# Second MLP product of tiles 0 to 7 as seven block products per tile pair

## The chip, the cores and the metric

The kernel runs on one core of a Trainium2 chip. The metric is device time in microseconds of one execution, as the median of several runs. The core has a matrix engine (TensorE, PE in the profile, with its weight loads listed as PEld), VectorE (DVE), ScalarE (ACT), GpSimd (POOL) and SyncE (SP, which issues DMAs). Each engine works through its own queue in order; semaphores make one engine wait for another. Matmuls write to PSUM, which is used here in banks of 512 fp32 values per partition; all other data lies in SBUF.

## The reference, cut to what matters

Two parts work on the same normalized input: an attention block with cached keys and values, and an MLP mixer whose output gates the attention.

```python
xn = _layernorm(x)                                  # 2048 x 512
s  = attention(xn, k_cache, v_cache, wq, wo)        # 32 heads, Dh 128, 2048 keys
# mixer on xn:
h  = _gelu(_layernorm(xn) @ w1)                     # then shifted by rows, in four column groups
x1 = xn + shifted(h) @ w2
h2 = _gelu(_layernorm(x1) @ w3) @ w4                # 512 -> 1792 -> 512
g  = _silu(x1 + h2)
return x + s * g
```

The product with `w4` is the second MLP product of the title. Its input has 2048 rows of 1792 values, its output 2048 rows of 512.

## The kernel before, in words

All tokens are cut into 16 tiles of 128 rows; four tiles make a chunk of 512 rows. `xall` holds the tiles' running values (x, then x1, then x1 + h2, then the gate) in bf16, tile by tile.

The order of the work is written out by hand: every instruction goes through `pin(...)`, which keeps the program's order on its engine, and the tile framework adds the semaphore waits from reads and writes of tiles. A PSUM tile fills a bank (or half of one), and an access of one engine to it waits for the other engines' accesses to the same tile, whichever half they touch. No planner with costs or due times takes part in the stage of the change.

The program begins with the mixer. It normalizes and transposes the tiles, then runs `m1` (product with w1, gelu), `m2` (shifted product with w2) and `x1` (adding it into `xall`), `ln2` (second normalization, on VectorE, with a DMA transpose into `xn2T`), and then the MLP:

- `m3(c, f)` makes 256 of the 1792 hidden columns of chunk `c`, transposed: eight matmuls of 512 columns into one two-bank PSUM tile, then one gelu on ScalarE into `h2`. Seven calls make a chunk.
- `m4(t, ps, fcs)` makes the second MLP product of tile `t`: for each of 14 blocks of 128 hidden columns one matmul, with the block of `h2` (128 x 128) as weights and the matching 128 rows of `w4` (512 columns) streamed. It sums in one PSUM bank.
- `x2` adds that bank into `xall` on VectorE. `gate_tanh` takes tanh of half of it on ScalarE, and `gate_silu` multiplies on VectorE.

The stage runs as: `m3` of chunks 0 and 1, then `gate_out` (m4, x2, tanh, silu) of tiles 0 to 3, `m3` of chunk 2, `gate_out` of tiles 4 to 7, `m3` of chunk 3. During this SyncE issues the loads of w4, of the first keys and values and of the first output weights `wo`. The pool `pL` is then closed and its memory goes to `pB`, which holds `wo` and the attention's tiles. The second product of tiles 8 to 15 follows one matmul at a time inside the attention's first slots (`held_mm`, with the same `m4`).

The rest, over a thousand microseconds, is the attention: per unit (head and 512 queries) eight slots of score matmuls, exp on ScalarE, value matmuls, and sums of exp on VectorE. The projection of queries there already uses seven block products in place of eight (`w_sum`, `x_sum`, `product`, `q_take`, `q_part`), whose rows of the profile serve as prices in the prediction.

In the profile every matmul carries line 112, that of the helper `mm`, so matmuls are told apart by the tiles they write and read: `ps_o<-w_sb,h2T` is the second MLP product of tiles 0 to 7, `ps_m<-w_sb,h2T` that of tiles 8 to 15, and `ps_s<-xn2T,w_sb` is `m3`. Line 293 is the gelu of `m3`, 302 is `x2`, 306 is tanh, 310 is the silu, 219 a normalization, 796 the load of `w4`, 516 that of `wo`. In the query projection line 405 is a ScalarE copy of the first block product, and lines 413 to 421 are VectorE adds; 442 to 455 are the attention's sums of exp.

Of the kernel before, what the change touches and what calls it, by code (L numbers as in the profile page):

```python
# [8 lines left out]
ACT = mybir.ActivationFunctionType  # L9
ALU = mybir.AluOpType  # L10
FP32 = mybir.dt.float32
BF16 = mybir.dt.bfloat16
# [5 lines left out]
def kernel(  # L18
# [15 lines left out]
    nc = tc.nc  # L34
    P = nc.NUM_PARTITIONS
# [3 lines left out]
    Sq, D = x2d.shape  # L39
    _, H, Sk, Dh = A_k_cache.shape  # L40
# [5 lines left out]
    DC = D // P  # L46
    KC = Sk // P
    FC = F // P
# [11 lines left out]
    PADW = 8  # L60
    PSUM = bass.MemoryType.PSUM
    pin = tc.keep_in_program_order

    def pool(name, bufs=1, space=None, **kw):
        if space is not None:
            kw["space"] = space
        return tc.tile_pool(name=name, bufs=bufs, **kw)
# [4 lines left out]
    xall = const.tile([P, NT, D], BF16, name="xall")  # L72
# [22 lines left out]
    psO = ent(pool("psO", 2, PSUM))  # L95
    psX = ent(pool("psX", 1, PSUM))
# [4 lines left out]
    pR = right.enter_context(pool("pR", side="right", reuse_waits="tile"))  # L101
    left = ExitStack()
    pL = left.enter_context(pool("pL", reuse_waits="tile"))
# [7 lines left out]
    def mm(out, lhsT, rhs, start, stop, **kw):  # L111
        pin(nc.tensor.matmul(out=out, lhsT=lhsT, rhs=rhs, start=start, stop=stop, **kw))  # L112
# [8 lines left out]
        out=ident[:], in0=diag[:], scalar1=0.0, scalar2=None, op0=ALU.is_equal))  # L121
# [9 lines left out]
    kTs, vBs, wqs, wos, oTs, st = {}, {}, {}, {}, {}, {}  # L131
# [37 lines left out]
    def token(early, name):  # L169
        if early:  # L170
            return pL.tile([P, D], BF16, tag="xi", bufs=5, name=name)
        return tokp.tile([P, D], BF16, tag="ta", bufs=6, name=name)
# [9 lines left out]

    w1_sb = pL.tile([P, DC, D], BF16, name="w1_sb")
    w2_sb = pL.tile([P, DC, D], BF16, name="w2_sb")
    w3_sb = [pL.tile([P, DC, 2 * P], BF16, name=f"w3_sb{i}") for i in range(FC // 2)]
    hT = pL.tile([P, DC, Sq + PADW], BF16, name="hT")
    xn2T = {}
    w4_sb = [pR.tile([P, D], BF16, name=f"w4_sb{i}") for i in range(FC)]  # L190
    h2 = {}

    def power(out, ve):
# [74 lines left out]
    def m2(t, pl=psO, tag="ps_o"):  # L268
        ps = pl.tile([P, D], FP32, tag=tag, name="ps_o")
        for jc in range(DC):  # L270
            c0 = BASE_J[jc] + t * P - SHIFT[jc]
            mm(ps[:], hT[:, jc, c0:c0 + P], w2_sb[:, jc, :], jc == 0, jc == DC - 1)
        return ps
# [12 lines left out]
    def m3(c, f):  # L286
        ps = psS.tile([P, 2, 512], FP32, name="ps_s")
        for j in range(2):
            for dc in range(DC):
                mm(ps[:, j, :], w3_sb[f][:, dc, j * P:(j + 1) * P], xn2T[c][:, dc, :],  # L290
                   dc == 0, dc == DC - 1)
        h2[c, f] = pR.tile([P, 2, 512], BF16, tag="h2T", bufs=FC, name="h2T")
        pin(nc.scalar.activation(out=h2[c, f][:], in_=ps[:], func=ACT.Gelu_apprx_tanh))  # L293

    def m4(t, ps, fcs):
        c, ts = divmod(t, 4)
        for fc in fcs:
            mm(ps[:], h2[c, fc // 2][:, fc % 2, ts * P:(ts + 1) * P], w4_sb[fc][:],
               fc == 0, fc == FC - 1)

    def x2(t, ps):
        pin(nc.vector.tensor_tensor(out=xall[:, t, :], in0=ps[:], in1=xall[:, t, :], op=ALU.add))

    def gate_tanh(t):
        th = token(False, "th")
        pin(nc.scalar.activation(out=th[:], in_=xall[:, t, :], func=ACT.Tanh, scale=0.5))
        return th

    def gate_silu(t, th):
        pin(nc.vector.scalar_tensor_tensor(  # L310
            out=xall[:, t, :], in0=th[:], scalar=1.0, in1=xall[:, t, :], op0=ALU.add, op1=ALU.mult))
# [29 lines left out]
    def x_block(qt, half, dcs):  # L341
        c = qt * 512 + 256 * half
        return xnT[:, dcs, c:c + 256]
# [23 lines left out]
    def product(v, k):  # L367
        g, qt, hh = units[v]
        h = g * HG + hh
        s = sw.setdefault(v, {})  # L370
        if k in (1, 7):
            s["ps"] = psX.tile([P, 2, 256], FP32, tag="xa", name="ps_q")
        w, o = wc[h], [wc[h][:, i] for i in range(4)]
        b11, _, b21, b22 = (wqs[h + j][:, d, :] for d in (LO, HI) for j in (0, 1))
        side, x, b = {
            1: (0, x_block(qt, 0, LO), b11),
            2: (0, x_block(qt, 0, HI), b21),
            3: (1, xs[qt, 3], b22),
            4: (0, x_block(qt, 1, HI), o[3]),
            5: (1, xs[qt, 0], o[0]),  # L380
            6: (1, xs[qt, 1], o[1]),
            7: (0, xs[qt, 2], o[2]),
        }[k]
        for dc in range(2):
            mm(s["ps"][:, side, :], b[:, dc, :], x[:, dc, :], k in (1, 7) and dc == 0, True, skip_group_check=True)
# [296 lines left out]
    for jc in range(DC):  # L682
        b = BASE_J[jc]
# [78 lines left out]
    for u in range(HG, 2 * HG):  # L762
        q_ahead(u)
    pend = [(3, m2(3))]
    wqs[H - 1] = pL.tile([P, DC, Dh], BF16, name="wq_e")
    pin(nc.sync.dma_start(out=wqs[H - 1][:], in_=wq_v[:, :, (H - 1) * Dh:]))
    for t in range(12, 16):
        ln1(t, tr_dma)
# [24 lines left out]
        elif t < 13:  # L793
            ln2(t - 5)
    for i in range(FC):
        pin(nc.sync.dma_start(out=w4_sb[i][:], in_=B_w4[i * P:(i + 1) * P, :]))
    for t in range(8, 12):
        stats(xall[:, t, :], mv2, rs2, t)
    for h in range(HG):
        load_k(h, range(KSPLIT))  # L800
        load_v(h, (0, 1))
        if h == 0:
            for f in range(FC // 2):
                m3(0, f)
            for t in range(12, 16):
                stats(xall[:, t, :], mv2, rs2, t)
            for t in range(8, 12):
                ln2(t)
        if h == 1:
            for f in range(FC // 2):  # L810
                m3(1, f)
            for t in range(12, 16):
                ln2(t)

    def gate_out(t):
        ps = psO.tile([P, D], FP32, tag="ps_o", name="ps_o")
        m4(t, ps, range(FC))
        x2(t, ps)
        gate_silu(t, gate_tanh(t))

    for t in range(0, 4):
        gate_out(t)
    for f in range(FC // 2):
        m3(2, f)
    for t in range(4, 8):
        gate_out(t)
    for f in range(FC // 2):
        m3(3, f)
    left.close()
    pB = left.enter_context(pool("pB", reuse_waits="tile"))  # L830

# [5 lines left out]
    for g in range(NG - 1):  # L837
        b = (g * QT + QT - 1) * HG
# [18 lines left out]
    def held_mm(n):  # L857
        for _ in range((4, 10)[n] if n < 2 else 3 if n < SPU + 2 else 2 if n < 2 * SPU else 1 + (n % SPU in (1, 5, 7))):
            if not held:
                return  # L860
            t, fc = held.popleft()
            if fc == 0:
                heldps[t] = psX.tile([P, 512], FP32, tag=("xa", "xm")[t % 2], name="ps_m")
            m4(t, heldps[t], (fc,))
            if fc == FC - 1:
                held_out(t, n)
# [34 lines left out]
    for v in pairs:  # L901
        a = (v - 2) * SPU
# [19 lines left out]
    for h in range(HG, H, 2):  # L922
        u = (h // HG) * QT * HG + (-4, -2)[h % HG // 2]
# [8 lines left out]
    for n in range(UB * SPU):  # L932
        u, p = divmod(n, SPU)
# [72 lines left out]
    n = UB * SPU  # L1006
    t0 = 4 * (QT - 1)
    ps, tb, yl, whole = {}, {}, {}, {}
# [25 lines left out]
    def pv_to(k):  # L1034
# [29 lines left out]
        out=diag[:], in0=diag[:], scalar1=0.0, scalar2=None, op0=ALU.is_equal))  # L1064
# [98 lines left out]
```

## Time and profile before

| | |
|---|---|
| median of 3 runs | 1235.81 us (1235.81 to 1235.9) |
| the profiled execution, whole | 1236.42 us |
| its span, first to last instruction | 1234.6 us |
| TensorE's granted clock | 1.0 |
| DMA moved | 107.75 MB, mean 87 GB/s |

The page lists for each engine its busy time and share of the span, then the granted clock in 40 slices, then the chain of work that ended last, by engine. A row of a group reads: line, engine, operation, tiles written and read, shapes, count, busy microseconds in all, mean nanoseconds of one, and the idle time ahead of it with the engine that ended it. A row of the timeline reads: start in the span, duration, engine, line, operation, tiles, count; equal instructions in a row are merged into one with their count. A row of the windows reads: window, its length, then busy time and count of PE, PEld, DVE, ACT and POOL, the granted clock, the DMA share and GB/s. The end of a matmul is modelled, and a matmul's listed duration overlaps the next one's.

### The profile page before, as it was taken

Reading aid. Unit: us, or ns where it says so; the run is one execution under the profiler, and the core shown is the slowest. Engines: PE = TensorE matmul, PEld = TensorE weight load, DVE = VectorE, ACT = ScalarE, POOL = GpSimd, SP = SyncE. Lnnn points to the kernel's source line nnn. Section 1 sums busy time; section 2 is a strip of 40 time slices with the busy share of each in tenths; the row PEclk is TensorE's granted clock in tenths of the full one; section 3 lists DMA queues with packets and bytes.
Section 4 is the critical chain, followed back from the end, with each engine's and each line's share of the span. In section 5 each row is a group of like instructions: output and inputs, shape, how many; then the busy total and the mean of one; then the engine's idle time right before and its main releaser. Section 6 shows DMA issues by size and latency. Waiting matters only on the chain.

```text
span 1234.6 us, 17534 instructions
## 1 busy us (share of the span) xinstructions
PE 1227.5 (99%) x6267; PEld 636.5 (52%) x6267; DVE 1030.1 (83%) x1647; ACT 1105.8 (90%) x1237; POOL 26.6 (2%) x75
## 2 busy tenths in 40 slices
PE   9999999999999999999999999999999999999998
PEld 6444444455555555555555555555555555555545
DVE  7712778899888888988889888888889999999997
ACT  6345999899999999999999999999999999999996
POOL 5300000000000000000000000000000000000000
PEclk9999999999999999999999999999999999999999
DMA  8661122664334423354243523543345424553342
GB/s 176 168 140 35 31 39 65 96 99 94 63 80 100 106 57 82 87 111 85 58 95 91 111 56 69 103 104 72 76 83 111 107 58 90 99 107 66 77 81 66
DMA packets 244056, 107.75 MB, mean 87 GB/s; under 512 B 194816, under 2 KB 227712, under 8 KB 243968
## 3 DMA queue, kind: packets, MB, share of 16 engines
q1 hardware_dynamic: 243408, 106.17, 41.5%
q8 instruction: 49, 0.80, 0.3%
q10 hardware_dynamic: 560, 0.46, 0.1%
q14 instruction: 39, 0.32, 0.1%
HBM read 67.50 MB, written 2.36 MB: 57 GB/s over the span
## 4 chain that ended last, share of the span: by engine, by line
PE 94%; DVE 3%; DMA 2%; ACT 1%; issue 0%; SPq 0%; DVEq 0%; ACTq 0%
PE ps_s L112 39%; PE ps_o L112 37%; PE ps_wo L112 8%; PE ps_q L112 8%; PE ps_m L112 2%; DMA tT<-acc 1%; DVE acc L447 1%; ACT pT L436 1%; DMA rb<-dr 0%; DMA xin<-in_A_x_dram 0%; DVE sm L485 0%; PE ps_oh L112 0%; DVE oT L509 0%; DVE acc L451 0%; DVE y L1025 0%
## 5 line engine op out<-in xcount | busy, mean ns | idle before, releaser
L436 ACT ACTIVATE pT<-ps_s 128x1024 bf16<-128x1024 f32 x1016 | 1016.2, 1025 | 56.8 <-PE ps_s L112 26.1
L112 PE MATMUL ps_s<-qT,kT 128*128 128x512 bf16 (+1 forms) x2064 | 609.3, 378 | 0.0
L112 PE MATMUL ps_o<-pT,vb 128*128 128x512 bf16 x1984 | 590.2, 379 | 0.0
L447 DVE TENSOR_TENSOR acc<-acc,pT 128x2048 bf16<-128x2048 bf16 x254 | 307.0, 1208 | 54.9 <-ACT pT L436 54.4
L112 PEld LDWEIGHTS <-kT 128*128 128x128 bf16 x2064 | 232.7, 113 | 151.3 <-issue 1.0
L112 PEld LDWEIGHTS <-vb 128*128 128x128 bf16 x1984 | 193.9, 98 | 216.6
L442 DVE TENSOR_TENSOR acc<-pT 128x2048 bf16<-128x2048 bf16 x127 | 155.4, 1224 | 38.4 <-ACT pT L436 35.5
L112 PE MATMUL ps_wo<-wo_h,oT 128*128 128x512 bf16 x496 | 186.3, 379 | 0.0
L451 DVE TENSOR_TENSOR acc<-acc 128x1024 bf16<-128x1024 bf16 x127 | 87.4, 688 | 2.5
L509 DVE TENSOR_TENSOR oT<-ps_o,rb 128x512 bf16<-128x512 f32 x127 | 86.6, 682 | 1.1 <-DMA rb<-dr 0.8
L485 DVE TENSOR_REDUCE sm<-tT 128x4 f32<-128x512 bf16 x124 | 83.9, 676 | 2.8 <-DMA tT<-acc 2.7
L112 PEld LDWEIGHTS <-oT 128*128 128x128 bf16 x528 | 51.4, 98 | 52.6 <-issue 0.6
L112 PEld LDWEIGHTS <-wc 128*128 128x128 bf16 x440 | 43.0, 98 | 54.1 <-issue 2.7
L571 DVE TENSOR_TENSOR sacc<-ps_wo,sacc 128x512 f32<-128x512 f32 x96 | 65.7, 684 | 0.0
L112 PEld LDWEIGHTS <-wq_h 128*128 128x128 bf16 x398 | 38.9, 98 | 46.3
L112 PE MATMUL ps_q<-xnT,wq_h 128*128 128x256 bf16 (+1 forms) x288 | 61.1, 298 | 0.4 <-DVE sacc L559 0.4
L421 DVE TENSOR_TENSOR qT<-ps_q,tq 128x512 bf16<-128x512 f32 x55 | 38.0, 692 | 23.3 <-PE ps_q L112 22.9
L455 DVE TENSOR_TENSOR acc<-acc 128x512 bf16<-128x512 bf16 x127 | 52.9, 417 | 0.5
L293 ACT ACTIVATE h2T<-ps_s 128x1024 bf16<-128x1024 f32 x28 | 28.6, 1023 | 25.9 <-PE ps_s L112 25.9
L112 PE MATMUL ps_s<-xn2T,w_sb 128*128 128x512 bf16 x224 | 48.8, 379 | 0.0
L112 PEld LDWEIGHTS <-w_sb 128*128 128x128 bf16 x368 | 33.5, 98 | 29.6
L112 PE MATMUL ps_q<-xs,wc 128*128 128x256 bf16 x246 | 47.0, 273 | 0.0
(102 smaller groups left out, 585.6 us busy)
## 6 DMA issues: line engine op xcount, KB each, us to landing
rb<-dr SPq DMA_DIRECT2D x127, 256.0 KB, 3.9
vb<-in_A_v_cache_dram SPq DMA_DIRECT2D x62, 256.0 KB, 3.0
wq_h<-in_A_wq_dram SPq DMA_DIRECT2D x32, 128.0 KB, 3.0
wo_h<-in_A_wo_dram SPq DMA_DIRECT2D x32, 128.0 KB, 2.5
w_sb<-in_B_w_dram SPq DMA_DIRECT2D x8, 256.0 KB, 5.0
kT<-in_A_k_cache_dram SPq DMA_TRANSPOSE x128, 2.8
xl<-in_A_x_dram SPq DMA_DIRECT2D x16, 128.0 KB, 3.0
dr<-rc SPq DMA_DIRECT2D x127, 2.0 KB, 1.4
```

The source lines that it names most:

```text
L112: pin(nc.tensor.matmul(out=out, lhsT=lhsT, rhs=rhs, start=start, stop=stop, **kw))
L293: pin(nc.scalar.activation(out=h2[c, f][:], in_=ps[:], func=ACT.Gelu_apprx_tanh))
L421: pin(nc.vector.tensor_tensor(out=s["q"][:, 1:3], in0=ps, in1=u.to_broadcast([P, 2] + list(u.shape[2:])), op=ALU.add))
L436: pin(nc.scalar.activation(out=s["pT"][-1][:, jj:jj + 2, :], in_=sps[:], func=ACT.Exp, scale=SCALE))
L442: pin(nc.vector.tensor_tensor(out=s["acc"][:], in0=s["pT"][0][:], in1=s["pT"][1][:], op=ALU.add))
L447: pin(nc.vector.tensor_tensor(out=a[:], in0=a[:], in1=st[u]["pT"][i][:], op=ALU.add))
L451: pin(nc.vector.tensor_tensor(out=a[:, 0:2, :], in0=a[:, 0:2, :], in1=a[:, 2:4, :], op=ALU.add))
L455: pin(nc.vector.tensor_tensor(out=a[:, 0, :], in0=a[:, 0, :], in1=a[:, 1, :], op=ALU.add))
L485: pin(nc.vector.tensor_reduce(out=sm[:], in_=s["tT"][:], axis=mybir.AxisListType.X, op=ALU.add))
L509: pin(nc.vector.tensor_tensor(out=to, in0=o, in1=rb, op=ALU.mult))
L571: pin(nc.vector.tensor_tensor(out=sa, in0=ps[:], in1=sa, op=ALU.add))
```

## The change

The second MLP product of tiles 0 to 7 is made for two tiles at a time, with four blocks on each side: the two tiles give the rows, the two 128-column halves of each hidden block give the inner halves (`k` = 0 and 1), and the left and right 256 columns of `w4` give the columns. Seven products of sums of blocks replace the eight products of blocks. The operand sums are made on VectorE: `t1` to `t4` from `w4` once, `s1` to `s4` from `h2` per pair (`h_sums`). Each product is seven matmuls of 256 columns that sum in PSUM; the products are then added up by eight VectorE adds and one copy on ScalarE per pair, which also bring in the residual from `xall`.

To be read in blocks, `w4` becomes one tile instead of 14, and `h2` one tile per chunk (two buffers) instead of 14 buffers of a seventh. The sums use memory whose first content is no longer needed: `hT` for the sums of `w4`, the `xp` buffers for the first pair of a chunk, and the `w1` and `w2` tiles for the second pair. For this some tiles get a tag. A pair's two fp32 work tiles, `mu` in the place of `wq_e` and `mt`, are used for nothing else at that time.

Within a pair the first product is copied by ScalarE after the second product has been issued into the other half of the same bank. For the second pair of a chunk, the gate of the first pair (two tanh, two silu) is issued between that copy and the pair's first add.

```diff
-    w1_sb = pL.tile([P, DC, D], BF16, name="w1_sb")
-    w2_sb = pL.tile([P, DC, D], BF16, name="w2_sb")
+    w1_sb = pL.tile([P, DC, D], BF16, tag="w1", bufs=1, name="w1_sb")
+    w2_sb = pL.tile([P, DC, D], BF16, tag="w2", bufs=1, name="w2_sb")
...
-    hT = pL.tile([P, DC, Sq + PADW], BF16, name="hT")
+    hT = pL.tile([P, DC, Sq + PADW], BF16, tag="hT", bufs=1, name="hT")
...
-    w4_sb = [pR.tile([P, D], BF16, name=f"w4_sb{i}") for i in range(FC)]
+    w4_sb = pR.tile([P, FC // 2, 2, D], BF16, name="w4_sb")
...
-        h2[c, f] = pR.tile([P, 2, 512], BF16, tag="h2T", bufs=FC, name="h2T")
-        pin(nc.scalar.activation(out=h2[c, f][:], in_=ps[:], func=ACT.Gelu_apprx_tanh))
+        if f == 0:
+            h2[c] = pR.tile([P, FC // 2, 2, 512], BF16, tag="h2T", bufs=2, name="h2T")
+        pin(nc.scalar.activation(out=h2[c][:, f], in_=ps[:], func=ACT.Gelu_apprx_tanh))
...
-            mm(ps[:], h2[c, fc // 2][:, fc % 2, ts * P:(ts + 1) * P], w4_sb[fc][:],
+            mm(ps[:], h2[c][:, fc // 2, fc % 2, ts * P:(ts + 1) * P], w4_sb[:, fc // 2, fc % 2, :],
...
-    wqs[H - 1] = pL.tile([P, DC, Dh], BF16, name="wq_e")
+    wqs[H - 1] = pL.tile([P, DC, Dh], BF16, tag="wqe", bufs=1, name="wq_e")
...
-        pin(nc.sync.dma_start(out=w4_sb[i][:], in_=B_w4[i * P:(i + 1) * P, :]))
+        pin(nc.sync.dma_start(out=w4_sb[:, i // 2, i % 2, :], in_=B_w4[i * P:(i + 1) * P, :]))
...
-    def gate_out(t):
-        ps = psO.tile([P, D], FP32, tag="ps_o", name="ps_o")
-        m4(t, ps, range(FC))
-        x2(t, ps)
-        gate_silu(t, gate_tanh(t))
-
-    for t in range(0, 4):
-        gate_out(t)
-    for f in range(FC // 2):
-        m3(2, f)
-    for t in range(4, 8):
-        gate_out(t)
-    for f in range(FC // 2):
-        m3(3, f)
+    w4t = pL.tile([P, 4, FC // 2, D // 2], BF16, tag="hT", bufs=1, name="w4t")
+    WL, WR = slice(0, D // 2), slice(D // 2, D)
+    b11, b12, b21, b22 = (w4_sb[:, :, k, c] for k in range(2) for c in (WL, WR))
+    t1, t2, t3, t4 = (w4t[:, i] for i in range(4))
+    for out, p, q in ((t1, b12, b11), (t2, b22, t1), (t3, b22, b12), (t4, b21, t2)):
+        pin(nc.vector.tensor_tensor(out=out, in0=p, in1=q, op=ALU.subtract))
+    hs = {}
+
+    def rows(t, k):
+        c, ts = divmod(t, 4)
+        return h2[c][:, :, k, ts * P:(ts + 1) * P]
+
+    def h_sums(t):
+        if t % 4 == 0:
+            hs[t] = [pL.tile([P, FC // 2, P], BF16, tag="xp", bufs=4, name="hs")[:] for _ in range(4)]
+        else:
+            two = [pL.tile([P, 2, FC // 2, P], BF16, tag=tag, bufs=1, name="hs") for tag in ("w1", "w2")]
+            hs[t] = [x[:, i] for x in two for i in range(2)]
+        s1, s2, s3, s4 = hs[t]
+        a11, a12, a21, a22 = (rows(t + r, k) for r in range(2) for k in range(2))
+        for out, p, q, op in ((s1, a21, a22, ALU.add), (s2, s1, a11, ALU.subtract),
+                              (s3, a11, a21, ALU.subtract), (s4, a12, s2, ALU.subtract)):
+            pin(nc.vector.tensor_tensor(out=out, in0=p, in1=q, op=op))
+
+    def flat(t, c0, n):
+        return xall[:].rearrange("p t d -> p (t d)")[:, t * D + c0:t * D + c0 + n]
+
+    def pair_out(t, between):
+        w = D // 2
+        s1, s2, s3, s4 = hs.pop(t)
+        a11, a12, _, a22 = (rows(t + r, k) for r in range(2) for k in range(2))
+        pa = psX.tile([P, 2, w], FP32, tag=("xa", "xm")[t % 4 // 2], name="ps_m")
+        pb, pc = (psO.tile([P, w], FP32, tag="ps_o", name="ps_o") for _ in range(2))
+
+        def product(out, a, b, start):
+            for f in range(FC // 2):
+                mm(out, a[:, f], b[:, f], start and f == 0, True, skip_group_check=True)
+
+        def add(out, p, q):
+            pin(nc.vector.tensor_tensor(out=out, in0=p, in1=q, op=ALU.add))
+
+        u = pL.tile([P, w], FP32, tag="wqe", bufs=1, name="mu")
+        ux = pL.tile([P, 2, w], FP32, tag="mt", bufs=1, name="mt")
+        product(pa[:, 0], a11, b11, True)
+        product(pa[:, 1], s2, t2, False)
+        pin(nc.scalar.activation(out=u[:], in_=pa[:, 0], func=ACT.Identity))
+        between()
+        add(u[:], pa[:, 1], u[:])
+        product(pb[:], s3, t3, True)
+        add(ux[:], u[:].unsqueeze(1).broadcast_to([P, 2, w]),
+            flat(t, w, 2 * w).rearrange("p (a c) -> p a c", a=2))
+        add(u[:], pb[:], u[:])
+        product(pc[:], s1, t1, True)
+        product(pa[:, 0], a12, b21, False)
+        add(u[:], u[:], flat(t + 1, w, w))
+        add(flat(t + 1, w, w), pc[:], u[:])
+        product(pb[:], a22, t4, False)
+        add(flat(t, 0, w), pa[:, 0], flat(t, 0, w))
+        product(pc[:], s4, b22, False)
+        add(flat(t + 1, 0, w), pb[:], ux[:, 1])
+        add(flat(t, w, w), pc[:], ux[:, 0])
+
+    def gate_pair(t):
+        th = [gate_tanh(t + i) for i in range(2)]
+        for i in range(2):
+            gate_silu(t + i, th[i])
+
+    for c in range(2):
+        h_sums(4 * c)
+        h_sums(4 * c + 2)
+        pair_out(4 * c, lambda: None)
+        pair_out(4 * c + 2, lambda: gate_pair(4 * c))
+        gate_pair(4 * c + 2)
+        for f in range(FC // 2):
+            m3(2 + c, f)
```

In the order of the products in `pair_out`, the prediction calls them P1 to P7; the first five VectorE adds after the copy are its a to e. The instructions of the attention and their order on every engine stay the same.

## The prediction

> **What bounds the kernel now.** I read the page first: which engine is full, at which clock, and what the chain that ended last is made of.
>
> ```profile
> span 1234.6 us, 17534 instructions
> PE 1227.5 (99%) x6267; PEld 636.5 (52%) x6267; DVE 1030.1 (83%) x1647; ACT 1105.8 (90%) x1237; POOL 26.6 (2%) x75
> PEclk9999999999999999999999999999999999999999
> PE 94%; DVE 3%; DMA 2%; ACT 1%; issue 0%; SPq 0%; DVEq 0%; ACTq 0%
> ```
>
> TensorE is busy 99% of the span at a clock granted in full, and 94% of the chain is its own. So a microsecond that TensorE gains or loses anywhere is a microsecond of the span, unless it stands idle later for something that has its own time. Next come the stages that the change touches, from the busy times by window, and the matmuls, gelus and gate steps there from the timeline.
>
> ```profile
> 69.50:81.60 12.10, 12.10 (x57) 5.49 (x56) 4.15 (x6) 2.91 (x4) 0.00 (x0) 1.00 0.80 127
> 93.70:105.80 12.10, 12.10 (x58) 5.47 (x57) 4.15 (x6) 2.91 (x4) 0.00 (x0) 1.00 0.22 71
> ...
> 69.53 12.25 PE L112 MATMUL ps_o<-w_sb,h2T 128*128 128x512 bf16 x56
> 69.73 1.02 ACT L293 ACTIVATE h2T<-ps_s 128x1024 bf16<-128x1024 f32 x1 [0.70 <-PE ps_s L112]
> 72.75 0.69 DVE L302 TENSOR_TENSOR xall<-ps_o,xall 128x512 bf16<-128x512 f32 x1 [17.32 <-PE ps_o L112]
> 73.48 0.63 ACT L306 ACTIVATE th<-xall 128x512 bf16<-128x512 bf16 x1 [2.73 <-DVE xall L302]
> 74.14 0.69 DVE L310 SCALAR_TENSOR_TENSOR xall<-th,xall 128x512 bf16<-128x512 bf16 x1 [0.70 <-ACT th L306]
> 81.62 12.25 PE L112 MATMUL ps_s<-xn2T,w_sb 128*128 128x512 bf16 x56
> ```
>
> The two windows are tiles 0 to 3 and 4 to 7 of the second product: TensorE is busy all 12.10 us of each, VectorE 4.15, ScalarE 2.91. The 56 matmuls start at 69.53 and the next group at 81.62, so four tiles take 12.09 us, 0.216 a matmul, and no matmul waits. The gate of a tile (add, tanh, multiply) runs beside the matmuls of the next tile; nothing behind it holds TensorE.
>
> **What is removed and what comes, on TensorE.** A pair of tiles had 28 matmuls of 512 columns; it gets seven products of 7 matmuls of 256 columns, 49. The price of a 256-column matmul with its own weights is in the first MLP stage:
>
> ```profile
> 16.79 3.66 PE L112 MATMUL ps_s<-xnT,w_sb 128*128 128x256 bf16 x32
> L112 PE MATMUL ps_s<-xnT,w_sb 128*128 128x256 bf16 x64 | 7.3, 273 | 0.0
> ```
>
> The last of the 32 shows 0.273 us, so 31 steps take 3.39: 0.109 a step, and a product of seven 0.765. A pair is 49 x 0.109 = 5.35 us against 28 x 0.216 = 6.04: 0.69 less, 2.75 for four pairs, if nothing waits.
>
> **What comes on VectorE ahead of the pairs.** Four differences of w4 (1792 elements a row), and eight sums of h2 (896 elements) per 512 rows.
>
> ```profile
> L447 DVE TENSOR_TENSOR acc<-acc,pT 128x2048 bf16<-128x2048 bf16 x254 | 307.0, 1208 | 54.9 <-ACT pT L436 54.4
> L451 DVE TENSOR_TENSOR acc<-acc 128x1024 bf16<-128x1024 bf16 x127 | 87.4, 688 | 2.5
> L356 DVE TENSOR_TENSOR xs<-xnT 128x512 bf16<-128x512 bf16 x5 | 2.1, 419 | 0.0
> L455 DVE TENSOR_TENSOR acc<-acc 128x512 bf16<-128x512 bf16 x127 | 52.9, 417 | 0.5
> ...
> L796 SPq DMA_DIRECT2D w_sb<-in_B_w_dram x14: 328/431/2406, 47.1 to 55.7; - x14
> DMA to landing us min/median/max: 2.2/2.5/4.7
> ...
> 52.79 2.64 DVE L219 TENSOR_SCALAR xn<-xall,mv,rs 128x512 bf16<-128x512 bf16 x8
> 57.64 1.02 ACT L293 ACTIVATE h2T<-ps_s 128x1024 bf16<-128x1024 f32 x1 [0.70 <-PE ps_s L112]
> ```
>
> Between 1024 and 2048 elements an element costs 0.51 ns, between 512 and 1024 0.53, so a difference takes 1.08 us and a sum 0.62. L356 reads runs of 256 out of a wider tile at the price of L455, so the strides of w4 and h2 should cost nothing. VectorE is free from 55.43; w4 has landed at 58.2 (60.4 with the longest landing), h2 of the first 512 rows stands at 58.7. Differences and sums take 4.4 and 5.2 us with their gaps: done at 67.8, at 70.0 at worst. The first sum is needed by the second product (70.3), and the VectorE behind them at 71.7: hidden. The next 512 rows' sums lie under 12 us of matmuls of the first product (81.62 row). Without that cover they would cost their 5.2 us.
>
> **What comes inside a pair.** Products P1 and P2 fill the two halves of one bank; a copy on ScalarE takes P1, and the built program lets it wait for P2's last matmul; add a (VectorE) forms the sum u of both; P3 and P4 fill two other banks. Then b makes two sums of u with the residual (512 elements), c adds P3, d the residual, e adds P4. P5 waits for a (same bank), P6 for c, P7 for e. In the second pair of each 512 rows the gate of the first pair stands ahead: two tanh behind the copy on ScalarE, two multiplies ahead of a on VectorE. Prices:
>
> ```profile
> L405 ACT ACTIVATE tq<-ps_q 128x256 f32<-128x256 f32 x55 | 21.6, 392 | 0.0
> L413 DVE TENSOR_TENSOR tq<-ps_q,tq 128x256 f32<-128x256 f32 x55 | 23.0, 418 | 0.0
> L421 DVE TENSOR_TENSOR qT<-ps_q,tq 128x512 bf16<-128x512 f32 x55 | 38.0, 692 | 23.3 <-PE ps_q L112 22.9
> L306 ACT ACTIVATE th<-xall 128x512 bf16<-128x512 bf16 x16 | 10.0, 626 | 19.8 <-DVE xall L302 19.8
> L310 DVE SCALAR_TENSOR_TENSOR xall<-th,xall 128x512 bf16<-128x512 bf16 x16 | 11.0, 689 | 5.7 <-ACT th L306 5.7
> ...
> 44.61 1.88 DVE L276 TENSOR_TENSOR xall<-ps_o,xall 128x512 bf16<-128x512 f32 x3
> 1063.76 0.42 DVE L418 TENSOR_TENSOR qT<-ps_q,tq 128x256 bf16<-128x256 f32 x1
> 1064.23 0.38 PE L112 MATMUL ps_q<-xnT,wc 128*128 128x256 bf16 x2 [0.98 <-DVE qT L418]
> 1214.08 1.22 DVE L447 TENSOR_TENSOR acc<-acc,pT 128x2048 bf16<-128x2048 bf16 x1
> 1215.33 0.69 DVE L451 TENSOR_TENSOR acc<-acc 128x1024 bf16<-128x1024 bf16 x1
> 128.02 0.68 DVE L302 TENSOR_TENSOR xall<-ps_m,xall 128x512 bf16<-128x512 f32 x1
> 128.85 1.23 DVE L447 TENSOR_TENSOR acc<-acc,pT 128x2048 bf16<-128x2048 bf16 x1
> ```
>
> Hand-overs: TensorE to VectorE 0.04 (69.53, 13 steps of 0.216 and the 0.38 of a matmul make 72.71; L302 starts at 72.75); VectorE to ScalarE and back 0.03 to 0.04 (L302, L306, L310 above); VectorE to a waiting matmul 0.05 (1064.18 to 1064.23); an add behind the one it needs 0.03 (1215.30 to 1215.33); independent ones overlap by 0.08 (three of 0.68 in 1.88). c and e wait for VectorE and TensorE both, as L447 does for two engines; it starts 0.15 behind L302 here, an upper end as it may have waited for exp. I take 0.07 for c and e, ends 0.03 and 0.15.
>
> First pair, from its start: P2 done at 13 x 0.109 + 0.273 = 1.69, copy 1.73 to 2.12 (the last gelu, 69.73 row, has left ScalarE at 1.22), a 2.16 to 2.58, b to 3.30, c to 3.79, d to 4.24, e to 4.73. P5 and P6 (due 3.06 and 3.83) start on time within 0.01; P7 would start at 4.60 and waits for e till 4.78. The pair ends at 4.78 + 0.765 = 5.54.
>
> Second pair: copy to 2.12, tanh 2.12 to 2.75 and to 3.38, multiplies 2.78 to 3.47 and 3.41 to 4.10, a only 4.02 to 4.44, b to 5.16, c to 5.65, d to 6.10, e to 6.59. P5 is due at 3.06 and starts at 4.49; P6 at 5.70, P7 at 6.64; end 7.40. The gate, free before, now costs the 1.86 us by which a comes later. What is late next is the pair's own gate and the gelus of the next product: the last adds end at 8.0, two tanh at 9.3, when the first gelu is due (7.40 + 8 x 0.216 + 0.16 + 0.04 = 9.3): no wait on TensorE, whose third group needs that gelu at 10.9.
>
> Two pairs: 12.94 against 12.09, 0.85 more; twice: **1.7 us slower**. With 0.03 and 0.15 for c and e (twice in each of four pairs) it is 1.4 and 2.4.
>
> **What else moves.** The weight tiles of the second pair's sums are reused for wo, so its first four loads (from 92.7 on before) now wait for the fourth pair's matmuls, to about 108. Behind them SyncE has the first turned sums, and wo is used later still:
>
> ```profile
> L516 SPq DMA_DIRECT2D wo_h<-in_A_wo_dram x8: 422/432/566, 92.7 to 198.9; - x8
> L480 SPq DMA_TRANSPOSE tT<-acc x3: 1200/1215/1225, 131.3 to 150.8; - x3
> L112 PE MATMUL ps_wo<-wo_h,oT x28: 378/379/380, 193.9 to 236.7; 128*128 128x512 bf16 x28
> ```
>
> Free by 23 us; uncovered, the first turned sums would wait for the issues, 0.43 each. All other transfers keep their order and waits, and what follows is shifted as a whole.
>
> The profiled execution took 1236.42 us around its span of 1234.6, the median of the runs is 1235.81. The sum against the span gives 1236.3, against the median **1237.5**.
>
> **Rivals.**
>
> 1. *Slower than 0.2%: late adds in the chain b to e.* Place: c and e of every pair, eight in all, each ahead of a product that waits. The 0.15 row speaks for it, the 0.03 row against. If each starts 0.25 behind instead of 0.07: 8 x 0.18 = 1.4 more, 1238.9. It passes 0.2% from 0.17 on.
>
> 2. *The clock falls.* The second pairs hold TensorE idle for 1.4 + 0.4 + 0.2 us. Before, its longest wait in the stream is 0.98 us, and the window around it keeps its clock:
>
> ```profile
> 1062.00:1066.00 4.00, 3.02 (x17) 1.58 (x16) 4.00 (x9) 2.74 (x3) 0.00 (x0) 1.00 0.41 64
> ```
>
> If longer waits halve it for P5 to P7, these take 21 x 0.109 = 2.3 more; 0.6 of it replaces waits; two such pairs cost 3.3: 1240.8. [...]
>
> 3. *The strided sums go at the four-byte rate* (L413 to L421: 1.07 ns an element): 2.06 and 1.10 each, 17 us from 58.2, so a of the first pair starts at 75.3, not 71.7: 3.6 more, once, 1241.1. L356 speaks against it.
>
> 4. *Less is lost.* If later idle time takes up half or more of the loss: 1235.8 to 1236.7. Of waits that could take it up there is little: the largest group in the list of waits, over the whole span, is
>
> ```profile
> PE ps_q L112 <- DVE qT L418: 1.4, 3, 1.0
> ```
>
> If nothing waits in the pairs, the whole gain comes: 1233.1; the order of the gate ahead of a speaks against it.
>
> **How the numbers follow.** My sum 0.47; rival 1 0.26, rival 2 0.08, rival 3 0.07, rival 4 0.08 for the partial and 0.04 for the whole gain. About 0.2% (2.5 us) is what a measurement of this kernel can tell from no change: faster 0.04, within 0.47 + 0.08 = 0.55, slower 0.26 + 0.08 + 0.07 = 0.41. The likeliest case alone spans 1237.2 to 1238.2; the range goes down into the partial case and up through rival 1: 1236.0 to 1239.6, leaving rivals 2 and 3 and the whole gain outside.
>
> **What would show it.** The matmuls of tiles 0 to 3 should take about 12.9 us from their first to the next product's first, with waits of TensorE for VectorE of 0.2 in first pairs and 2.0 in second ones (1.4 ahead of P5). Twelve wide VectorE sums before 70 us at 1.08 and 0.62 show the hidden part right; a first add later than 71.7 shows rival 3; a granted clock below 1.00 rival 2; c or e over 0.1 behind the instruction ahead rival 1. The prediction is wrong if a second pair takes under 6.5 or over 8.2 us, or if the stages after 130 us shift by another amount than this one.

## The result, and the profile after

| | before | after |
|---|---|---|
| median of 22 runs | 1235.82 us (1235.16 to 1236.9) | 1238.07 us (1237.18 to 1238.45) |
| profiled execution, whole | 1236.42 us | 1237.74 us |
| its span | 1234.6 us | 1236.0 us |
| granted clock | 1.0 | 1.0 |

The ratio is 1.0017, with a 95% interval of 1.001 to 1.0023: 2.25 us slower, between 1.2 and 2.8. The ratio itself lies within 0.2% of no change; its interval reaches a little past that. Forecast were 1237.5 us and a loss of 1.7. (Of the 20 executions of the kernel before that were timed with the second group of experiments below, one was slow, with 2649.92 us, and the ratios leave it out.)

The page of the changed kernel answers the first lines quoted of before. (Some matmul records are missing in this trace, so the counts of PE are a little low.)

```profile
span 1236.0 us, 17643 instructions
...
PE 1220.7 (99%) x6234; PEld 645.8 (52%) x6351; DVE 1051.0 (85%) x1691; ACT 1106.7 (90%) x1241; POOL 26.5 (2%) x75
...
PEclk9999999999999999999999999999999999999999
...
PE 93%; DVE 4%; ACT 1%; issue 1%; DMA 1%; DVEq 0%; ACTq 0%
```

VectorE has 21 us more work and 44 more instructions. In the chain of waits one per cent of the span has gone from TensorE to VectorE. Where that is, the list of TensorE's waits in the stage says (microseconds in all, times, the longest):

```profile
PE ps_m L112 <- DVE mu L855: 2.3, 2, 1.1
PE ps_o L112 <- DVE mu L855: 0.6, 2, 0.3
```

Both stand on adds of the second pairs. (The list counts a wait from the modelled end of the last matmul, so it shows less than start against due time.) The busy times by window, cut at each pair's first matmul and at the next product's, give the lengths:

```profile
69.59:75.22 5.63, 5.57 (x50) 4.78 (x49) 3.06 (x7) 1.41 (x2) 0.00 (x0) 1.00 0.64 163
75.22:82.57 7.35, 5.85 (x52) 4.69 (x49) 4.68 (x10) 1.42 (x3) 0.00 (x0) 1.00 0.97 102
94.66:100.28 5.62, 5.56 (x50) 4.78 (x49) 3.05 (x7) 1.41 (x2) 0.00 (x0) 1.00 0.00 0
100.28:107.63 7.35, 5.84 (x51) 4.69 (x49) 4.69 (x10) 1.42 (x3) 0.00 (x0) 1.00 0.07 18
```

A pair took 6.04 us before. First pairs take 0.4 less, second pairs 1.3 more, at a clock of 1.00 in all. Two such pairs make 0.89, the two chunks 1.78. Here is a second pair in the timeline, matmuls, ScalarE and VectorE in order of time:

```profile
76.75 1.69 PE L112 MATMUL ps_o<-w4t,hs 128*128 128x256 bf16 x14
76.95 0.38 ACT L861 ACTIVATE mu<-ps_m 128x256 f32<-128x256 f32 x1 [5.25 <-PE ps_m L112]
77.23 1.14 ACT L307 ACTIVATE th<-xall 128x512 bf16<-128x512 bf16 x2
77.88 1.29 DVE L311 SCALAR_TENSOR_TENSOR xall<-th,xall 128x512 bf16<-128x512 bf16 x2 [2.04 <-ACT th L307]
79.09 0.42 DVE L855 TENSOR_TENSOR mu<-ps_m,mu 128x256 f32<-128x256 f32 x1
79.55 0.69 DVE L855 TENSOR_TENSOR mt<-mu,xall 128x512 f32<-128x512 f32 x1
79.57 0.94 PE L112 MATMUL ps_m<-w_sb,h2T 128*128 128x256 bf16 x7 [1.13 <-DVE mu L855]
80.34 0.42 DVE L855 TENSOR_TENSOR mu<-ps_o,mu 128x256 f32<-128x256 f32 x1
80.80 0.42 DVE L855 TENSOR_TENSOR mu<-mu,xall 128x256 f32<-128x256 f32 x1
80.82 0.92 PE L112 MATMUL ps_o<-w4t,h2T 128*128 128x256 bf16 x7 [0.31 <-DVE mu L855]
81.33 0.42 DVE L855 TENSOR_TENSOR xall<-ps_o,mu 128x256 bf16<-128x256 f32 x1
81.81 0.93 PE L112 MATMUL ps_o<-w_sb,hs 128*128 128x256 bf16 x7
```

P3 and P4 are the 14 matmuls at 76.75; P5 is due 14 steps later, at 78.28, and starts at 79.57, when a (79.09) has ended. P6 follows c (80.34) and P7 follows e (81.33). Add a has stood behind the two multiplies, and these behind the two tanh.

Which of the three waits sets the pair's length follows from the same rows. Counted from the pair's start at 75.22, P5 starts at 4.35 with three products of 0.765 to go, which alone would end the pair at 6.65; P6 starts at 5.60 with two to go (7.13) and P7 at 6.59 with one to go (7.35). The last is the pair's length.

Further down the whole program is shifted by what the stage lost. First the matmuls with wo, in the kernel before and then in the changed one (median time of one, then the first and the last start):

```profile
L112 PE MATMUL ps_wo<-wo_h,oT x28: 378/379/380, 193.9 to 236.7; 128*128 128x512 bf16 x28
```

```profile
L112 PE MATMUL ps_wo<-wo_h,oT x27: 378/379/379, 195.7 to 238.6; 128*128 128x512 bf16 x27
```

And a scaling on VectorE near the end, by its line, again before and changed:

```profile
L537 DVE SCALAR_TENSOR_TENSOR sacc<-sacc,xall x8: 684/684/686, 941.0 to 1062.2; 128x512 f32<-128x512 f32 x8
```

```profile
L538 DVE SCALAR_TENSOR_TENSOR sacc<-sacc,xall x8: 683/684/685, 942.9 to 1063.3; 128x512 f32<-128x512 f32 x8
```

The shift is 1.8 to 1.9 us at 194, 237 and 941 us; in the last of these rows, at 1062, it is 1.1, and the spans of the two profiled executions differ by 1.4. The stage explains 1.8 of the runs' 2.25. The rest lies within the interval, but no trace shows it; the last section returns to what happens behind 1000 us.

### The profile page after: what moved, and what is told of

The parts are those of the page before. It is cut to its first block, busy times and chain, and to the rows that moved or that the text cites. A ratio compares the mean times of both kernels' runs of the same rounds, so it can differ in the third digit from the quotient of the medians.

```text
span 1236.0 us, 17643 instructions
## 1 busy us (share of the span) xinstructions
PE 1220.7 (99%) x6234; PEld 645.8 (52%) x6351; DVE 1051.0 (85%) x1691; ACT 1106.7 (90%) x1241; POOL 26.5 (2%) x75
## 4 chain that ended last, share of the span: by engine, by line
PE 93%; DVE 4%; ACT 1%; issue 1%; DMA 1%; DVEq 0%; ACTq 0%
PE ps_s L112 39%; PE ps_o L112 35%; PE ps_q L112 8%; PE ps_wo L112 8%; PE ps_m L112 3%; DMA tT<-acc 1%; DVE acc L448 1%; ACT pT L437 1%; PE ps_warm L112 0%; DVE mu L855 0%; DVE mt L855 0%; PE ps_oh L112 0%; DVE sm L486 0%; DVE xall L311 0%; DVE y L1087 0%
## 5 line engine op out<-in xcount | busy, mean ns | idle before, releaser
L112 PE MATMUL ps_o<-pT,vb 128*128 128x512 bf16 x1908 | 573.5, 379 | 3.2
L448 DVE TENSOR_TENSOR acc<-acc,pT 128x2048 bf16<-128x2048 bf16 x254 | 306.9, 1208 | 55.7 <-ACT pT L437 55.4
L112 PE MATMUL ps_wo<-wo_h,oT 128*128 128x512 bf16 x475 | 178.2, 379 | 0.1
```

The costliest lines, as they stand in the source:

```text
L448: pin(nc.vector.tensor_tensor(out=a[:], in0=a[:], in1=st[u]["pT"][i][:], op=ALU.add))
```

## The experiments

The theory was the prediction's sum: the narrow matmuls give 2.75 us, and the waits of P5 to P7 behind the chain a to e, above all behind the gate ahead of a, take more than that away. Each kernel was timed against the kernel before on the same chip, in one of two groups; that kernel's median was 1236.55 us in the first group (e1 to e4) and 1236.68 in the second. Differences are to the kernel before of the same group; the changed kernel stands at +2.25 in its own. The ratios are not those of the two medians, so the last two columns can differ a little, most of all in e7 with its five runs.

| run | first / second pair, us | median, us | to before | ratio, 95% interval |
|---|---|---|---|---|
| changed kernel | 5.63 / 7.35 | 1238.07 | +2.25 | 1.0017 [1.001, 1.0023] |
| e1 multiplies last | 5.62 / 5.63 | 1235.03 | -1.52 | 0.9986 [0.9978, 0.9995] |
| e2 chain short too | 5.36 / 5.34 | 1233.98 | -2.57 | 0.9979 [0.9968, 0.9989] |
| e3 layout alone | four tiles 12.09 | 1236.65 | +0.10 | 0.9997 [0.9989, 1.0006] |
| e4 two banks | 5.35 / 6.58 | 1236.36 | -0.19 | 0.9996 [0.9987, 1.0005] |
| e5 one multiply ahead | 5.63 / 6.75 | 1237.09 | +0.41 | 1.0006 [0.9997, 1.0015] |
| e6 chain short, gate ahead | 5.35 / 6.65 | 1236.54 | -0.14 | 1.0 [0.999, 1.0009] |
| e7 sums longer | 9.32 / 7.35 | 1242.04 | +5.36 | 1.0053 [1.0039, 1.0067] |

### e1: the gate's multiplies behind the pair

```diff
-        pair_out(4 * c + 2, lambda: gate_pair(4 * c))
-        gate_pair(4 * c + 2)
+        th = {}
+        pair_out(4 * c + 2, lambda: th.update({t: gate_tanh(t) for t in (4 * c, 4 * c + 1)}))
+        for t in (4 * c + 2, 4 * c + 3):
+            th[t] = gate_tanh(t)
+        for t in range(4 * c, 4 * c + 4):
+            gate_silu(t, th[t])
```

> The two tanh of a chunk's first pair stay behind the copy, but its two multiplies go behind the second pair's last add. Theory (the gate ahead of add a is what makes the second pairs long): a starts 1.8 us earlier, second pairs take what first pairs take, 5.63 us instead of 7.35, and the time falls by 2 x 1.72 = 3.4 us against the changed kernel, 1.7 under the kernel before. Rival (the wait is due to the copy behind P2 or to the sums, and the multiplies only fill it): second pairs stay above 7 us and the time within 0.5 us of the changed kernel.

Measured: second pairs 5.63 us, 1.5 us under the kernel before, 3.8 under the changed one by the two differences. Second pair of the first chunk in its timeline:

```profile
76.94 0.38 ACT L861 ACTIVATE mu<-ps_m 128x256 f32<-128x256 f32 x1 [5.24 <-PE ps_m L112]
77.22 1.14 ACT L307 ACTIVATE th<-xall 128x512 bf16<-128x512 bf16 x2
77.36 0.42 DVE L855 TENSOR_TENSOR mu<-ps_m,mu 128x256 f32<-128x256 f32 x1 [1.52 <-ACT mu L861]
78.27 0.93 PE L112 MATMUL ps_m<-w_sb,h2T 128*128 128x256 bf16 x7
79.09 0.92 PE L112 MATMUL ps_o<-w4t,h2T 128*128 128x256 bf16 x7
80.08 0.93 PE L112 MATMUL ps_o<-w_sb,hs 128*128 128x256 bf16 x7
80.84 12.25 PE L112 MATMUL ps_s<-xn2T,w_sb 128*128 128x512 bf16 x56
```

The copy and both tanh stand where they stood, add a starts 0.04 behind the copy, and P5 starts when due. So what makes a second pair longer than a first one is the multiplies queued ahead of a on VectorE; the tanh cost something only where a multiply ahead of a waits for them (e5). The copy behind P2 alone does not do it; what it costs when the gate stands behind it is the subject of e4.

### e2: the same, and add b out of the chain

The diff to e1:

```diff
         product(pb[:], s3, t3, True)
-        add(ux[:], u[:].unsqueeze(1).broadcast_to([P, 2, w]),
-            flat(t, w, 2 * w).rearrange("p (a c) -> p a c", a=2))
-        add(u[:], pb[:], u[:])
+        v = pL.tile([P, w], FP32, tag="xi", bufs=5, name="mv")
+        add(v[:], pb[:], u[:])
         product(pc[:], s1, t1, True)
         product(pa[:, 0], a12, b21, False)
-        add(u[:], u[:], flat(t + 1, w, w))
-        add(flat(t + 1, w, w), pc[:], u[:])
+        add(v[:], v[:], flat(t + 1, w, w))
+        add(flat(t + 1, w, w), pc[:], v[:])
+        add(ux[:], u[:].unsqueeze(1).broadcast_to([P, 2, w]),
+            flat(t, w, 2 * w).rearrange("p (a c) -> p a c", a=2))
         product(pb[:], a22, t4, False)
```

> As the run with the multiplies last, and in every pair the 512-element add b moves behind add e (c writes a tile of its own). Theory (the rest is the chain a to e): e ends 0.7 us earlier, P6 and P7 start when due, every pair takes 49 x 0.109 = 5.36 us, and TensorE's whole gain comes: 2.7 us under the kernel before, 5.0 under the changed one. Rival (the narrow matmuls don't hold 0.109 us when their weights change at each step and the sums come from VectorE, or the loss is found after 130 us): pairs stay at 5.6 us, or the stage is shorter and the time isn't.

Measured: 2.57 us under the kernel before. The windows of its four pairs:

```profile
69.67:75.03 5.36, 5.36 (x51) 4.80 (x50) 2.96 (x7) 1.41 (x2) 0.00 (x0) 1.00 0.62 164
75.03:80.37 5.34, 5.34 (x51) 4.78 (x49) 3.38 (x8) 1.42 (x3) 0.00 (x0) 1.00 0.99 120
92.46:97.81 5.35, 5.35 (x51) 4.79 (x49) 2.96 (x7) 1.41 (x2) 0.00 (x0) 1.00 0.13 41
97.81:103.16 5.35, 5.35 (x52) 4.79 (x49) 3.38 (x8) 1.42 (x3) 0.00 (x0) 1.00 0.08 25
```

TensorE is busy for the whole of each, 49 steps of 0.109, with weights changed at every step and operands made by VectorE. This is the fastest of the kernels timed here. A ratio of 1 lies outside its interval, as it does for e1.

### e3: the layout alone

The diff is the changed kernel's own for the tiles of `w4` and `h2` and the tags; the stage below it is `gate_out` and `m3` as in the kernel before.

> The new layout of w4 and h2 (one tile each) and the tags, with the 14 matmuls of 512 columns a tile and the gate as before: no block products, no sums. Theory: the layout costs nothing, four tiles take 12.09 us, the time is that of the kernel before within 0.5 us. Rival (coarser tiles make later waits, for w4 as a whole or for the memory of the closed pool): some of the 2.2 us stay, above 0.7 us over the kernel before.

Measured: no difference that can be told. Its matmuls:

```profile
69.66 12.25 PE L112 MATMUL ps_o<-w_sb,h2T 128*128 128x512 bf16 x56
81.75 12.25 PE L112 MATMUL ps_s<-xn2T,w_sb 128*128 128x512 bf16 x56
```

From 69.66 to 81.75 are the same 12.09 us as before. The coarser tiles and the new tags cost nothing.

### e4: P1 and P2 in banks of their own

```diff
-        pa = psX.tile([P, 2, w], FP32, tag=("xa", "xm")[t % 4 // 2], name="ps_m")
+        pa, pd = (psX.tile([P, w], FP32, tag=tag, name="ps_m") for tag in ("xa", "xm"))
...
-        product(pa[:, 0], a11, b11, True)
-        product(pa[:, 1], s2, t2, False)
+        product(pa[:], a11, b11, True)
+        product(pd[:], s2, t2, True)
-        pin(nc.scalar.activation(out=u[:], in_=pa[:, 0], func=ACT.Identity))
+        pin(nc.scalar.activation(out=u[:], in_=pa[:], func=ACT.Identity))
         between()
-        add(u[:], pa[:, 1], u[:])
+        add(u[:], pd[:], u[:])
...
```

> P1 and P2 in banks of their own, everything else as in the changed kernel: the copy waits for P1 alone and P5 for the copy alone. Theory: first pairs 5.36 us; in second pairs the copy ends at 1.4 instead of 2.1, the gate and a come 0.75 earlier, P6 at 4.95, P7 at 5.9, end 6.65. Chunks 12.0 instead of 12.98, 1.9 us under the changed kernel, within 0.3 of the kernel before. Rival (the wait of P5 for a, in the shared bank, is what costs, 1.13 us in the list of waits): second pairs fall by that 1.1 and by the 0.75, to 5.5, and the time by 3.7.

Measured: second pairs 6.58 us, 0.77 shorter, as the theory has it, and not the rival's 5.5. P5 now starts when due, and the wait has gone to P6:

```profile
77.99 0.93 PE L112 MATMUL ps_m<-w_sb,h2T 128*128 128x256 bf16 x7
79.77 0.92 PE L112 MATMUL ps_o<-w4t,h2T 128*128 128x256 bf16 x7 [0.85 <-DVE mu L855]
80.75 0.93 PE L112 MATMUL ps_o<-w_sb,hs 128*128 128x256 bf16 x7
```

P5's wait, the largest in the list of waits, was not what the pair's length hung on: P6 and P7 would have waited for c and e anyway. From the pair's start at 74.93, P7 starts at 5.82, and with its 0.765 that makes the 6.58. What the shared bank costs is the 0.765 us by which it holds the copy, and with it the gate.

### e5: one multiply ahead of a

The diff is that of e1, with the first of the chunk's four `gate_silu` back in `between`, behind both tanh.

> Both tanh and only one of the two multiplies stay ahead of add a in second pairs; the other goes behind the pair. Theory (each instruction ahead of a costs its time, through the chain a to e): a ends at 3.7 instead of 4.3 us from the pair's start, the second pair takes 6.75 instead of 7.35, twice 0.6: 1.2 us under the changed kernel, 0.6 over the kernel before. Rival (ScalarE's tanh or the copy holds a, not the multiplies): no change, 7.35.

Measured: second pairs 6.75 us, between 5.63 (no multiply ahead) and 7.35 (two). The time is 0.4 over the kernel before, with an interval from -0.4 to +1.9 that also holds the expected 0.6; the pair's length in the trace is the sharper evidence. The first multiply costs 1.12 us, the second 0.60. The first costs more than its own 0.69 because it waits for tanh:

```profile
78.44 0.69 DVE L311 SCALAR_TENSOR_TENSOR xall<-th,xall 128x512 bf16<-128x512 bf16 x1 [2.04 <-ACT th L307]
79.05 0.42 DVE L855 TENSOR_TENSOR mu<-ps_m,mu 128x256 f32<-128x256 f32 x1
79.52 0.94 PE L112 MATMUL ps_m<-w_sb,h2T 128*128 128x256 bf16 x7 [0.53 <-DVE mu L855]
```

Add a starts 3.27 us into this pair (75.78), against 2.15 in e1 and 3.87 in the changed kernel.

### e6: the short chain with the gate ahead

The diff is that shown for e2, on the changed kernel, with its gate left where it was.

> The gate stays ahead of a as in the changed kernel; only add b moves behind e, and c writes a tile of its own. Theory: first pairs 5.36 us, second pairs a at 4.3, P6 at 4.9, P7 at 5.8, end 6.6; chunks 12.0, 2.0 us under the changed kernel and 0.2 under the kernel before. Rival (P5's wait for a sets the second pair's length): first pairs gain their 0.27, second pairs stay near 7.3, 0.6 under the changed kernel.

Measured: 5.35 and 6.65 us, 2.4 us under the changed kernel by the two differences. P5 waits for a as long as in the changed kernel (1.13 us of it in the list of waits), and yet the second pair is 0.70 shorter:

```profile
79.31 0.94 PE L112 MATMUL ps_m<-w_sb,h2T 128*128 128x256 bf16 x7 [1.13 <-DVE mu L855]
80.08 0.93 PE L112 MATMUL ps_o<-w4t,h2T 128*128 128x256 bf16 x7
80.84 0.93 PE L112 MATMUL ps_o<-w_sb,hs 128*128 128x256 bf16 x7
```

P6 and P7 now follow P5 without a gap. Here it is P5's wait that sets the length: from the pair's start at 74.96, P5 starts at 4.35 as in the changed kernel, and three products of 0.765 make 6.65. So the same wait counts for nothing extra in the changed kernel, where the adds c and e end later still, and for everything once they don't. With e4 this shows that a pair's length is the largest, over P5, P6 and P7, of the time at which its add lets it start plus the products from there on; the longest single wait need not be the one that gives it.

### e7: the cover of the sums

```diff
-        h_sums(4 * c + 2)
+        for _ in range(5 if c == 0 else 1):
+            h_sums(4 * c + 2)
```

> The changed kernel with the four sums of h2 for the first chunk's second pair made five times over (the same values into the same tiles): 9.3 us more of VectorE ahead of the first pair. Theory (the sums are hidden under 6.2 us in which VectorE idled before the first add a, and cost one for one beyond it): a of the first pair starts at 74.85 instead of 71.74, the time is 3.1 us over the changed kernel. Rival (the sums disturb TensorE or the transfers while they run): more than 4 us, or matmuls of the first product slower than 0.216 us.

Measured: 5.36 us over the kernel before, 3.1 over the changed one by the medians; but the interval is 4.8 to 8.3 over the kernel before, too wide to tell 3.1 from the rival's 4. The trace has to decide. Its first pair in the timeline:

```profile
75.77 0.42 DVE L855 TENSOR_TENSOR mu<-ps_m,mu 128x256 f32<-128x256 f32 x1
76.24 0.93 PE L112 MATMUL ps_m<-w_sb,h2T 128*128 128x256 bf16 x7 [3.10 <-DVE mu L855]
```

And by their tile, the matmuls of the first product that ran beside the sums:

```profile
L112 PE MATMUL ps_s<-xn2T,w_sb x66: 379/379/380, 54.8 to 68.8; 128*128 128x512 bf16 x66
```

From 54.8 to 68.8 us these are 65 steps of 0.215, so the matmuls beside the sums keep their pace. (The sums of `h2` run from 61.68 on.) In this execution the pair is 3.7 us longer rather than 3.1: VectorE's first difference started 0.75 later than in the changed kernel (57.55 against 56.80), the pair itself 0.33 later (69.92 against 69.59), and the 16 added sums took 9.5 instead of 9.3. With that the sums cost one for one beyond the idle time, and nothing within it. What they do to the transfers stays open.

## Why the prediction was right

**The gain on TensorE** was 0.69 us a pair: e2 has it whole, 5.35 against 6.04.

**The sums hidden.** A difference took 1.09 and a sum 0.62, as priced. The differences began at 56.80, earlier than the 58.2 assumed, as the loads of w4 had been issued by 54.8 instead of 55.7, and the sums were done at 65.55, 2.3 before the forecast. VectorE then idled 6.2 us before the first a. First difference, last sum and first a in the changed kernel's timeline:

```profile
56.80 1.09 DVE L821 TENSOR_TENSOR w4t<-w_sb 128x1792 bf16<-128x1792 bf16 x1 [1.31 <-issue]
...
64.93 0.62 DVE L838 TENSOR_TENSOR hs<-h2T,hs 128x896 bf16<-128x896 bf16 x1
71.74 0.43 DVE L855 TENSOR_TENSOR mu<-ps_m,mu 128x256 f32<-128x256 f32 x1 [6.19 <-ACT mu L861]
```

Rival 3, the strided sums at 1.07 ns an element (2.06 and 1.10 us each), is out by these rows, and e7 shows what the cover was worth.

**The chain in a pair.** Forecast 5.54 and 7.40, measured 5.63 and 7.35. Two prices were a little off, in opposite directions. Adds that wait for two engines' semaphores (c and e) start 0.10 behind the add that they need, not the 0.07 taken, within its ends of 0.03 and 0.15. The rows of the changed kernel's first pair, in order b, c, d, e:

```profile
72.20 0.69 DVE L855 TENSOR_TENSOR mt<-mu,xall 128x512 f32<-128x512 f32 x1
72.99 0.42 DVE L855 TENSOR_TENSOR mu<-ps_o,mu 128x256 f32<-128x256 f32 x1
73.45 0.43 DVE L855 TENSOR_TENSOR mu<-mu,xall 128x256 f32<-128x256 f32 x1
73.98 0.42 DVE L855 TENSOR_TENSOR xall<-ps_o,mu 128x256 bf16<-128x256 f32 x1
```

(72.20 + 0.69 to 72.99, and 73.45 + 0.43 to 73.98; the plain one, c to d, is 0.04.) Rival 1 supposed 0.25, so it is out, though its sign (over 0.1) was set so low that the measured 0.10 stands right at it. And the first tanh starts 0.10 before the copy ahead of it has ended (76.95 + 0.38 against 77.23), which is most of the reason why a came at 3.87 from the pair's start, not 4.02. In the second pair the two nearly cancel, so that it came out within 0.05 is in part luck.

**Where the time is lost.** The step that the prediction named, the gate ahead of a, is confirmed by e1 and, in its dose, by e5. That the pair's length comes through P6 and P7 was in its working; that P5's wait, the largest, could go without gain of its size came out in e4, and that it sets the length once c and e are earlier in e6.

**The clock** stayed at 1.00 through second pairs with waits of 1.3, 0.5 and 0.2 us in 7.35 (P5 to P7, start against due time), so rival 2 is out. In e7's first pair P5 starts 3.3 us after it is due (76.24 against 72.98); its seven matmuls take 0.93 us there too, and the mean clock of that execution is 0.999. The halving that rival 2 supposed, with its 2.3 us for P5 to P7, is in none of these pairs: a clock of 0.50 stands in the changed kernel's span only from 1235.4 us on, behind the last matmul, which starts at 1232.2.

**What else moves.** The first wo load went out at 103.5 and the next three from 107.8 on, close to the 108 forecast, instead of from 92.7 on; the matmuls that need them began 1.8 later like everything else: free, as said. Rival 4, a loss taken up later, had 1.8 us of shift kept to beyond 940 us against it. But the prediction also said that it is wrong if the stages after 130 us shift by another amount, and to the end that did not hold: the shift stayed to 1000 us and ended at 1.3 (last section).

The sum of 1.7 stands against 1.78 in the stage and 2.25 [1.2, 2.8] in the runs. The mechanism, the place and the size in the stage were right; the further 0.5 of the runs was not forecast, and no run explains it.

## What to carry to other kernels

Here fewer streamed columns on a full TensorE were worth all that they save, 0.69 us a pair, only where the adds that free the PSUM banks kept up (e2: 5.35 us a pair; the changed kernel: 5.63 and 7.35). To find out on paper, list, for each product, the add that it waits for, take the time at which that add lets it start plus the products still to come, and the largest of these is the length. Work of another tile belongs behind that chain in the add engine's queue, not inside it, even when it is ready (e1: second pairs 5.63 us in place of 7.35): here two multiplies and one wide add in the wrong place turned a gain of 2.6 us into a loss of 2.2. The longest wait in the list need not be the one that counts (e4: P5's 1.13 us gone, the pair 0.77 shorter); move it away on paper and see what waits next.

## What the runs showed of the hardware that was not expected

In the changed kernel the VectorE adds that need the add ahead of them and a product of TensorE (c and e) started 0.10 us behind the former, those that need only the add ahead (b and d) 0.03 to 0.04. Its trace shows what lies between: ahead of each of the eight adds c and e stands a wait instruction of its own (in the first pair at 72.93 and 73.92). It starts 0.04 behind the add before, takes 0.02, and the add starts another 0.04 behind it.

The shift did not stay constant to the end. ScalarE's exps come 1.84 to 1.85 us later in the changed kernel from 120 to 1000 us, and 1.3 at the end. In between, TensorE waits for VectorE in the query projection at other places. The kernel before waits 0.98 us at 1064.23 (the row is among the prediction's prices); the changed kernel does not wait there, but before it:

```profile
1048.50 0.38 PE L112 MATMUL ps_q<-xnT,wc 128*128 128x256 bf16 x2 [0.79 <-DVE qT L419]
```

With the layout alone (e3) the stage is as long as before, its list of waits has one of this kind, of 0.3 us, and the span is 0.9 us shorter. In the seven kernels with block products the lists have two each, the longest of 0.4 to 1.0. One execution of each kernel was traced, so whether the kernel or the execution sets these waits stays open. By its span, a single profile of this kernel therefore cannot be trusted with a change below about 1 us; the stage's own windows can.
